# A retention layer and a SwiGLU block on one core: rounding of weights without a sign operation, and vector work moved between VectorE and ScalarE

## The chip, the cores and the metric

The kernel runs on one core of a Trainium2 chip. A core has five engines that run beside each other and wait for each other by semaphores: TensorE (PE; its weight loads are shown as PEld), VectorE (DVE), ScalarE (ACT), GpSimd (POOL) and SyncE (SP). Each works through its instructions in their order. ACT and SP also issue the kernel's DMAs, each from its own instruction queue, so that a DMA issue that has to wait holds up what stands behind it. The metric is the device time of one execution in microseconds (us); less is better.

## The reference

Eight batches with eight heads of 576 positions and 64 columns each. A retention step with decay makes x of 4608 rows and 512 columns, and a feed-forward block with 1536 hidden columns works on x:

```python
scores = scale * np.matmul(q, k.transpose(0, 1, 3, 2))
gamma = 1.0 - 2.0 ** (-5.0 - np.arange(H))
Dmat = np.where(rel >= 0, gamma[:, None, None] ** rel[None, :, :], 0.0)   # rel = row - column
x = bridge(np.matmul(scores * Dmat, v))          # (B,H,S,D) -> (B*S, H*D)
g, val = x @ w_gate, x @ w_val
out = (g / (1 + np.exp(-g)) * val) @ w_out
```

q, k and v are float32. The three weight matrices come as float64.

## The kernel before, in words

**Head pairs and ticks.** The retention is done for one pair of heads at a time: 32 pairs (8 batches x 4). A position's decay is split into a factor for the key, a mask and a factor for the query, in chunks of 64 positions, with a running state for the chunks before. `tick(t)` (L540) puts three pairs in flight. On PE it issues `own_values` of pair t-2 (L434), `new_states` of pair t-1 (L443), `earlier_values` of pair t-2 (L453, L457) and `scores` of pair t-1 (L464, L470). The rest of a tick is a list of pieces that is worked off at once or one by one at later steps (`go_on`): first `copies` (L481, ACT, the even chunks' new states out of PSUM) together with `keys` (L415, ACT, the two heads' keys times their decay), then `both` (L504 and L518, DVE, the outputs out of PSUM times the query's factor, into x), then the masks and states (L477 to L492, DVE), and last the two transposes of q and k of pair t (L411, DVE). `load(i)` (L254) brings a pair's q, k and v with 14 DMAs on SP's queue; it comes two ticks ahead, and its q and k need a place that the transposes of an earlier pair set free.

**Weights.** Each float64 weight of 1 MB is loaded by ACT's queue (`load_w`, three places) and rounded to float32 in two halves. `split` (L364, L365, on ACT) makes a scaled float32 out of the upper 32 bits and an integer out of the lower ones. `rounding` (L377 to L380, on DVE) shifts the first left by three bits, puts the sign bit back and adds the second. There are 36 halves. The order of loads and roundings is written out by hand (`order`, `round_until`, L332 and L901), and each rounding issues the next split.

**Tiles of tokens.** The first tile has 512 tokens; the four after it have 1024. The first is done plainly: `up0(f)` for twelve steps (L574, PE L579, Silu L583 on ACT, product L584 on DVE), with the banks in two pairs that alternate between steps, then `down0(f)` for twelve (L589, PE L591), the plain output steps, then `out0` (L594) copies the four banks out and issues four DMAs. Ticks 4 to 9 lie between the up steps and ticks 10 to 13 between the down steps. The other tiles use a scheme with fewer products: 26 up steps for each quarter of the hidden columns and 26 down steps, whose operands are sums of weight blocks and of x blocks. The tables UP, DOWN and OUT_SUMS list these sums. The sums of the output weights (`out_sums`, L641; POOL, line L617 and its neighbours) are formed during the first tile and stored (`dn<-rest`, L668). The groups that come up to step 10 are stored from SP's queue at once, those from step 11 on from ACT's; the latter are held back in a list until `stores_until` lets them go. The sums of the up weights are made during the second tile (`w_sums`: POOL L617 and L781, ACT L780) and stored by ACT (L814), then fetched in the later tiles. The second tile thus has more vector work than the later ones. Its bank results are read by DVE (L752), ACT (L749, L826) and POOL, and the products of the hidden values are made by L829, L832 and L833. The ticks of pairs 12 to 19 are spread over the steps of the second tile.

These functions and some definitions around them are printed here with the line numbers that the profile uses.

Of the kernel before, what the change touches and what calls it, by code (L numbers as in the profile page):

```python
# [12 lines left out]
F32 = mybir.dt.float32  # L13
# [9 lines left out]
def tables(gamma, scale, L):  # L23

    g, at = np.array(gamma), np.arange(L)  # L30
    both = lambda t: np.repeat(t, L, axis=0).reshape(-1, 2 * L, t.shape[1]).transpose(1, 0, 2).reshape(2 * L, -1)
    twice = lambda t: np.concatenate([t, t])
    parts = [twice((g[:, None] ** -at).T), twice((g[:, None] ** (L - at)).T),
             both(g[:, None] ** L), both(g[:, None] ** (2 * L)), both(scale * g[:, None] ** at),
             both((scale * g[:, None] ** at).reshape(-1, 2, L)[:, ::-1].reshape(-1, L))]
    return np.concatenate(parts, axis=1).astype(np.float32)

# [113 lines left out]
def kernel(  # L151
# [144 lines left out]
    table = tables(gamma, scale, L)  # L296
    tab = const.tile(list(table.shape), F32, name="tab")
    decays = nc.inline_tensor(table, name="decays").ap()
    NCOL = 2 * H + 2 * HP
    nc.sync.dma_start(out=tab[:, 0:NCOL], in_=decays[:, 0:NCOL])  # L300
    load(0)
    load(1)
# [6 lines left out]
    step = tab[:, 2 * H : NCOL]  # L309
# [46 lines left out]
    def split(j):  # L356

        i, f = halves[j]  # L360
        bits = bits_of(i, f)
        top, ulp = [rest[:, part_at + 512 * (2 * n + j % 2) : part_at + 512 * (2 * n + j % 2 + 1)] for n in range(2)]
        blocks = lambda a: a.rearrange("p (c m) -> p c m", m=P)
        nc.scalar.activation(out=blocks(top), in_=bits[:, :, :, 1].bitcast(F32), func=AF.Copy, scale=2.0 ** -112)  # L364
        nc.scalar.activation(out=blocks(ulp.bitcast(I32)), in_=bits[:, :, :, 0].bitcast(U32), func=AF.Copy, scale=2.0 ** -29)  # L365
        parts[j] = top.bitcast(I32), ulp.bitcast(I32)
        if f and j // 2 + RAWS < len(order):
            load_w(j // 2 + RAWS)

    def rounding(j):  # L370

        i, f = halves[j]
        dst = weights[i][1][f].bitcast(I32)
        top, ulp = parts.pop(j)
        nc.vector.tensor_scalar(out=dst, in0=top, scalar1=3, scalar2=None, op0=ALU.logical_shift_left)  # L377
        nc.vector.scalar_tensor_tensor(out=top, in0=top, scalar=-(1 << 31), in1=dst,
                                       op0=ALU.bitwise_and, op1=ALU.bitwise_or)
        nc.vector.tensor_tensor(out=dst, in0=top, in1=ulp, op=ALU.add)  # L380
        if j + 1 < len(halves):
            split(j + 1)

# [6 lines left out]


    st = {}

    def transposes(i):
        p = i % HP
        qk, kn, vt, last = loaded.pop(i)
        qT = qp.tile([P, S], F32, tag="qT", name="qT")
        st[i] = dict(qT=qT, kn=kn, v=vt, last=last)
        pieces = []
        if i < HP:  # L400

            for t, src, bank in ((qT, qk[0], bankA), (kT, kn, bankB)):
                for c in range(NFULL):
                    nc.tensor.transpose(bank[:, ts(c, P)], src[:, c].rearrange("p h d -> p (h d)"), ident)
                nc.scalar.copy(out=t[:, 0:CW], in_=bank)
            nc.tensor.transpose(bankC[:, 0:P], qk[1].rearrange("p h d -> p (h d)"), ident)
            for n, t in enumerate((qT, kT)):
                nc.scalar.copy(out=t[:, CW:S], in_=bankC[:, n * L : (n + 1) * L])
        else:
            for n, t in enumerate((qT, kT)):  # L410
                pieces.append(lambda n=n, t=t: nc.vector.transpose(out=t, in_=qk[:, n].rearrange("p j d -> p (j d)")))  # L411

        def keys():
            for hl in range(2):
                nc.scalar.activation(out=kn[:, :, hl, :], in_=kn[:, :, hl, :], func=AF.Copy,  # L415
                                     scale=key[:, 2 * p + hl : 2 * p + hl + 1])
            if i < RAWS:
                load_w(i)

        return [keys] + pieces  # L420

    straight, exchanged = [(slice(0, P), slice(0, P))], [(half[0], half[1]), (half[1], half[0])]
# [50 lines left out]
    def masked(i):  # L473
        p = i % HP

        def own():
            nc.vector.tensor_tensor(out=ret, in0=sc, in1=near[:, 2 * p : 2 * p + 2].unsqueeze(2).to_broadcast([P, 2, NFULL, L]),  # L477
                                    op=ALU.mult)

        def copies():  # L480
            nc.scalar.copy(out=even, in_=z[:, 0])  # L481

        def states():

# [7 lines left out]
            nc.vector.scalar_tensor_tensor(out=at[:, :, 1], in0=at[:, :, 0], scalar=step[:, p : p + 1], in1=even,  # L492
                                           op0=ALU.mult, op1=ALU.add)

        return [copies, own, states]

    def to_x(i):
# [3 lines left out]

        def both():

            nc.vector.tensor_tensor(out=dst(NC - 1, NC), in0=xr, in1=qry[:, p], op=ALU.mult)  # L504
            lo = 0
            while lo < NC - 1:
                end = lo + 1
                while end < NC - 1 and where(end)[0] == where(lo)[0]:
                    end += 1
                for r in range(2):  # L510
                    cs = range(lo + (lo + r) % 2, end, 2)
                    if cs:
                        n = len(cs)
                        for src, to in (exchanged if r and x else straight):
                            at = dst(cs[0] - r, cs[0] - r + 2 * n) if cs[0] - r >= lo and cs[-1] + 2 - r <= end else None
                            if at is not None:
                                at = at[to].rearrange("p (c r i) -> p c r i", r=2, i=L)[:, :, r]
                                nc.vector.tensor_tensor(out=at, in0=xo[src, cs[0] // 2 : cs[0] // 2 + n, r],  # L518
                                                        in1=(qry_odd if r and x else qry)[src, p].unsqueeze(1).to_broadcast([at.shape[0], n, L]), op=ALU.mult)
                            else:  # L520
                                for c in cs:
                                    nc.vector.tensor_tensor(out=dst(c, c + 1)[to], in0=xo[src, c // 2, r], in1=(qry_odd if r and x else qry)[src, p], op=ALU.mult)
                lo = end

        def dst(lo, end):
# [68 lines left out]
    def out0():  # L594
        for i, bank in enumerate(banks):
            o = rest[:, part_at + 512 * i : part_at + 512 * (i + 1)]
            if i < 3:
                nc.vector.tensor_copy(out=o, in_=bank)  # L598
            else:
                nc.scalar.copy(out=o, in_=bank)  # L600
            nc.scalar.dma_start(out=out[i * P : (i + 1) * P, :], in_=o)


    up, down = lines(UP), lines(DOWN)
# [36 lines left out]
    def out_sums(qd):  # L641
# [21 lines left out]
        def do(k, late):  # L663
            e = events[k]
            if e[0] is None:
                _, slot, i = e
                src, queue = view(slot), nc.scalar if late else nc.sync
                waiting.append((place.get(slot), lambda: queue.dma_start(out=dn_ops[i][:, qd * TB : (qd + 1) * TB], in_=src)))  # L668
# [258 lines left out]
    for m, f in enumerate(down_order):  # L927
# [69 lines left out]
```

## Time and profile before

| | us |
|---|---|
| median of 4 runs | 1086.05 (1084.39 to 1087.93) |
| the profiled execution | 1084.39 |
| its span, first to last instruction | 1082.7 |
| PE busy in it | 1041.8 (96%) |
| DVE busy | 678.4 (63%) |
| ACT busy | 266.9 (25%) |
| POOL busy | 408.4 (38%) |

The profile is of one execution. A row of groups gives line, engine, operation, what it writes and reads by the program's names (out<-in), its shapes (partitions x elements), how often it comes, and then busy us, mean ns of one, and the idle time of the engine just before, with what ended it. A row of the timeline gives start and duration in us, and in brackets the idle time before it and its releaser. A row of waits gives the sum in us, the number of waits and the longest. SPq and ACTq are the queues' own instructions, such as DMA issues. Matmul ends are modelled, so the busy time of PE says that matmuls followed each other and not that each ran at its peak.

### The profile page before, as it was taken

The page shows a single profiled execution, that of the slowest core. Times are in us where ns is not written, and L with a number is a line of the kernel's source. Part 1 is how long each engine was busy: PE and PEld are TensorE (multiplying, and loading weights), DVE is VectorE, ACT ScalarE, POOL GpSimd, SP SyncE. Part 2 cuts the span into 40 slices and gives each one's busy share as a digit, 9 for nine tenths or more (in the row PEclk, how much of TensorE's full clock was granted, in tenths as well). Part 3 has the DMA queues.
Part 4 walks back from the last instruction along what each step waited for, and adds up shares of the span by engine and source line. Part 5 has one row for each costly group of instructions (what it writes and reads, how often), then busy time and mean ns, then how long its engine had stood idle before and what let it go on. Part 6 is the DMA issues. An engine that isn't in the chain of part 4 may idle for free.

```text
span 1082.7 us, 21505 instructions
## 1 busy us (share of the span) xinstructions
PE 1041.8 (96%) x8420; PEld 853.5 (79%) x8420; DVE 678.4 (63%) x1123; ACT 266.9 (25%) x560; POOL 408.4 (38%) x357
## 2 busy tenths in 40 slices
PE   5899889999989899999999999999999999999998
PEld 4545445678878788888888888888888888888887
DVE  1788974976887976754646868535267464244644
ACT  3455421223242211223232111122221012231110
POOL 1002459675546402641215025622151375122505
PEclk9899999999999999999999999999999999999999
DMA  8989966666657779767667678554565555555653
GB/s 210 225 216 229 247 174 203 194 193 181 172 167 194 236 195 247 208 181 192 146 176 217 175 195 245 149 155 136 156 169 158 160 175 154 153 150 156 183 167 98
DMA packets 304212, 198.58 MB, mean 183 GB/s; under 512 B 219632, under 2 KB 247280, under 8 KB 304112
## 3 DMA queue, kind: packets, MB, share of 16 engines
q1 hardware_dynamic: 272512, 152.80, 54.1%
q10 hardware_dynamic: 31600, 44.41, 12.4%
q8 instruction: 67, 1.10, 0.5%
q14 instruction: 33, 0.27, 0.1%
HBM read 157.04 MB, written 40.11 MB: 182 GB/s over the span
## 4 chain that ended last, share of the span: by engine, by line
PE 73%; DVE 8%; DMA 7%; POOL 5%; issue 3%; SPq 2%; ACT 1%; ACTq 0%; DVEq 0%; POOLq 0%
PE bankC L811 11%; PE bankE L811 10%; PE bankA L811 10%; PE bankB L811 10%; PE bankE L850 6%; PE bankB L850 6%; PE bankC L850 6%; PE bankA L850 6%; POOL rest L617 2%; DVE rest L752 2%; PE outer L457 1%; DMA v<-in_v_dram 1%; POOL arena L617 1%; DMA rest<-in_moe_w_out_dram 1%; PE outer L434 1%
## 5 line engine op out<-in xcount | busy, mean ns | idle before, releaser
L752 POOL TENSOR_TENSOR rest<-rest 128x512 f32<-128x512 f32 x56 | 79.1, 1419 | 297.4 <-DVE rest L752 279.0
L826 ACT ACTIVATE io<-rest 128x256 f32<-128x256 f32 x180 | 75.0, 417 | 349.3 <-DVE rest L752 306.5
L811 PE MATMUL bankA<-rest,arena 128*128 128x256 f32 x544 | 129.1, 380 | 3.7 <-DVE rest L598 1.8
L811 PE MATMUL bankC<-rest,arena 128*128 128x256 f32 x544 | 129.3, 380 | 2.3 <-DVE rest L752 1.4
L617 POOL TENSOR_TENSOR rest<-rest 128x256 f32<-128x256 f32 (+1 forms) x86 | 84.1, 999 | 124.4 <-DVE rest L380 96.3
L617 POOL TENSOR_TENSOR arena<-arena 128x512 f32<-128x512 f32 (+1 forms) x72 | 114.6, 1605 | 32.4 <-DMA up<-arena 19.2
L811 PE MATMUL bankB<-rest,arena 128*128 128x256 f32 x512 | 121.6, 380 | 1.7 <-DVE arena L829 0.8
L811 PE MATMUL bankE<-rest,arena 128*128 128x256 f32 x512 | 121.5, 380 | 0.6 <-DVE rest L752 0.6
L811 PEld LDWEIGHTS bankA<-rest,arena 128*128 128x128 f32 x544 | 102.8, 190 | 19.8 <-issue 5.2
L811 PEld LDWEIGHTS bankC<-rest,arena 128*128 128x128 f32 x544 | 102.7, 190 | 17.7 <-issue 2.6
L833 POOL TENSOR_TENSOR arena<-rest,io 128x256 f32<-128x256 f32 x72 | 51.9, 726 | 167.1 <-ACT io L826 167.1
L811 PEld LDWEIGHTS bankB<-rest,arena 128*128 128x128 f32 x512 | 96.8, 190 | 16.3 <-POOL arena L781 1.2
L811 PEld LDWEIGHTS bankE<-rest,arena 128*128 128x128 f32 x512 | 96.9, 190 | 14.6 <-DVE rest L752 1.0
L752 DVE TENSOR_TENSOR rest<-bankC,rest 128x512 f32<-128x512 f32 x72 | 48.9, 687 | 66.0 <-PE bankC L811 45.9
L752 DVE TENSOR_TENSOR rest<-bankE,rest 128x512 f32<-128x512 f32 x72 | 48.8, 685 | 65.3 <-PE bankE L811 47.1
L752 DVE TENSOR_TENSOR rest<-bankB,rest 128x512 f32<-128x512 f32 x72 | 48.8, 686 | 64.7 <-PE bankB L811 47.0
L752 DVE TENSOR_TENSOR rest<-bankA,rest 128x512 f32<-128x512 f32 x72 | 48.8, 685 | 62.7 <-PE bankA L811 45.8
L829 DVE SCALAR_TENSOR_TENSOR arena<-rest,io 128x256 f32<-128x256 f32 x84 | 53.4, 640 | 12.6 <-ACT io L826 12.6
L850 PE MATMUL bankB<-arena 128*128 128x256 f32 x252 | 58.3, 381 | 0.0
L850 PE MATMUL bankA<-arena 128*128 128x256 f32 x252 | 58.1, 380 | 0.0
L850 PE MATMUL bankC<-arena 128*128 128x256 f32 x252 | 58.0, 380 | 0.0
L850 PE MATMUL bankE<-arena 128*128 128x256 f32 x252 | 57.9, 379 | 0.0
(150 smaller groups left out, 1650.0 us busy)
## 6 DMA issues: line engine op xcount, KB each, us to landing
arena<-up SPq DMA_DIRECT2D x234, 256.0 KB, 2.7
arena<-dn SPq DMA_DIRECT2D x104, 384.0 KB, 3.6
up<-arena ACTq DMA_DIRECT2D x78, 256.0 KB, 3.1
out_dram<-rest SPq DMA_DIRECT2D x32, 256.0 KB, 3.4
qk<-in_q_dram SPq DMA_DIRECT2D x112, 72.0 KB, 3.3
qk<-in_k_dram SPq DMA_DIRECT2D x112, 72.0 KB, 3.3
v<-in_v_dram SPq DMA_DIRECT2D x62, 128.0 KB, 3.1
kn<-in_k_dram SPq DMA_DIRECT2D x58, 128.0 KB, 3.2
```

The costliest lines, as they stand in the source:

```text
L434: m = nc.tensor.matmul(xo[half[hl ^ r * exchange(i)], c, r], s["v"][half[r], c, hl, :], ret[half[r], hl, c], start=(c == 0), stop=(c == 0) ...
L457: nc.tensor.matmul(xr[half[hl]] if c + 1 == NC else xo[half[hl ^ c % 2 * exchange(i)], c // 2, c % 2], state[half[hl], c, :], s["qT"][half ...
L617: eng.tensor_tensor(out=dst, in0=srcs[0], in1=srcs[1], op=ALU.add if op[0] == "add" else ALU.subtract)
L752: eng.tensor_tensor(out=at(op[1]), in0=at(op[2]), in1=at(op[3]), op=ALU.add if op[0] == "add" else ALU.subtract)
L811: nc.tensor.matmul(b[:, gv * TB : (gv + 1) * TB], w[:, gv, ts(c, P)], rhs[:, c, :], start=(opens and gv == 0 and c == 0), stop=(c == 1), s ...
L826: nc.scalar.activation(out=s, in_=src[:, 0:TB], func=AF.Silu, scale=-1.0 if negative else 1.0)
L829: return lambda: nc.vector.scalar_tensor_tensor(out=dst, in0=src[:, TB : 2 * TB], scalar=-1.0, in1=s, op0=ALU.mult, op1=ALU.mult)
L833: nc.gpsimd.tensor_tensor(out=dst, in0=src[:, TB : 2 * TB], in1=s, op=ALU.mult)
L850: nc.tensor.matmul(b[:, m * TB : (m + 1) * TB], lhs[:, qd, ts(m, P)], w[:, qd], start=(opens and qd == 0 and m == 0), stop=(qd == NQ - 1), ...
```

## The change

Four things are changed. In the rounding, the operation that puts the sign back is taken out; the split reads the upper bits through a parametric relu (`Prelu`) whose slope for negative values is 2^32, which after the shift by three bits leaves a one in the sign's place. At ticks 10, 11 and 12 (`vector`), which lie between the plain output steps and just behind them, the keys' scaling and the copy of the even states are done by DVE and not by ACT. For pairs 12 to 19 (`light`), ACT scales q with the query's factor ahead of the transposes, by a table of factors (`piece`) that is loaded with the small tables, and the outputs are then only copied to x, by ACT, where DVE multiplied them. In `out0` ACT copies the first two banks and DVE the last two, and the four DMAs come after the copies. The stores of the output weights' sums on ACT's queue are held back by three from the start, where they were all held back until the second down step.

```diff
+    half = [np.repeat(g.reshape(-1, 2), L, axis=1).T ** (lane % 32 + 32 * r) for r in range(2)]
+    pieces = scale * np.stack(half, axis=2).reshape(2 * L, -1)
...
-    NCOL = 2 * H + 2 * HP
+    NCOL = 2 * H + 4 * HP
...
-        nc.scalar.activation(out=blocks(top), in_=bits[:, :, :, 1].bitcast(F32), func=AF.Copy, scale=2.0 ** -112)
+        nc.scalar.activation(out=blocks(top), in_=bits[:, :, :, 1].bitcast(F32), func=AF.Prelu, scale=2.0 ** -112, alpha=2.0 ** 32)
...
-        nc.vector.scalar_tensor_tensor(out=top, in0=top, scalar=-(1 << 31), in1=dst,
-                                       op0=ALU.bitwise_and, op1=ALU.bitwise_or)
-        nc.vector.tensor_tensor(out=dst, in0=top, in1=ulp, op=ALU.add)
+        nc.vector.tensor_tensor(out=dst, in0=dst, in1=ulp, op=ALU.add)
...
+    def light(i):
+        return needed(1) - 2 <= i < needed(2) - 2
+    def vector(i):
+        return 10 <= i <= needed(1) - 2
...
+            if light(i):
+                def scale_q():
+                    src = qk[:, 0].rearrange("p (j r) d -> p r j d", r=2)
+                    for r in range(2):
+                        nc.scalar.activation(out=src[:, r], in_=src[:, r], func=AF.Copy, scale=piece[:, 2 * p + r : 2 * p + r + 1])
+                pieces.append(scale_q)
...
+                if vector(i):
+                    nc.vector.tensor_scalar(out=kn[:, :, hl, :], in0=kn[:, :, hl, :],
+                                            scalar1=key[:, 2 * p + hl : 2 * p + hl + 1], scalar2=None, op0=ALU.mult)
...
+        if light(i):
+            return [lambda: (keys(), pieces[0]())] + pieces[1:]
...
-            nc.scalar.copy(out=even, in_=z[:, 0])
+            (nc.vector.tensor_copy if vector(i + 1) else nc.scalar.copy)(out=even, in_=z[:, 0])
...
-            nc.vector.tensor_tensor(out=dst(NC - 1, NC), in0=xr, in1=qry[:, p], op=ALU.mult)
+            if light(i):
+                nc.scalar.copy(out=dst(NC - 1, NC), in_=xr)
+            else:
+                nc.vector.tensor_tensor(out=dst(NC - 1, NC), in0=xr, in1=qry[:, p], op=ALU.mult)
...
-                for r in range(2):
+                for r in range(0 if light(i) else 2):
...
+                if light(i) and lo % 2 == end % 2 == 0:
+                    nc.scalar.copy(out=dst(lo, end).rearrange("p (c r i) -> p c r i", r=2, i=L), in_=xo[:, lo // 2 : end // 2])
...
-            if i < 3:
-                nc.vector.tensor_copy(out=o, in_=bank)
-            else:
-                nc.scalar.copy(out=o, in_=bank)
-            nc.scalar.dma_start(out=out[i * P : (i + 1) * P, :], in_=o)
+            (nc.vector.tensor_copy if i > 1 else nc.scalar.copy)(out=o, in_=bank)
+        for i in range(4):
+            nc.scalar.dma_start(out=out[i * P : (i + 1) * P, :], in_=rest[:, part_at + 512 * i : part_at + 512 * (i + 1)])
...
-    behind = [len(OUT_SUMS)]
...
-                stores_until(behind[0] if late else 0)
+                stores_until(3 if late else 0)
...
-                stores_until(behind[0], new)
+                stores_until(3, new)
...
-        if m == 1:
-
-            behind[0] = 3
-            stores_until(3)
```

More of the change, by code (lines that the diff above doesn't have):

```diff
@@ L30, in tables @@
     g, at = np.array(gamma), np.arange(L)
+    lane = np.arange(2 * L)[:, None]
     both = lambda t: np.repeat(t, L, axis=0).reshape(-1, 2 * L, t.shape[1]).transpose(1, 0, 2).reshape(2 * L, -1)
     twice = lambda t: np.concatenate([t, t])
+    half = [np.repeat(g.reshape(-1, 2), L, axis=1).T ** (lane % 32 + 32 * r) for r in range(2)]
+    pieces = scale * np.stack(half, axis=2).reshape(2 * L, -1)
     parts = [twice((g[:, None] ** -at).T), twice((g[:, None] ** (L - at)).T),
-             both(g[:, None] ** L), both(g[:, None] ** (2 * L)), both(scale * g[:, None] ** at),
+             both(g[:, None] ** L), both(g[:, None] ** (2 * L)), pieces, both(scale * g[:, None] ** at),
              both((scale * g[:, None] ** at).reshape(-1, 2, L)[:, ::-1].reshape(-1, L))]
@@ L308 @@
     inv, key = tab[:, 0:H], tab[:, H : 2 * H]
-    step = tab[:, 2 * H : NCOL]
+    step = tab[:, 2 * H : 2 * H + 2 * HP]
+    piece = tab[:, NCOL - 2 * HP : NCOL]
     qry, qry_odd = [tab[:, NCOL + HP * L * n : NCOL + HP * L * (n + 1)].rearrange("p (h i) -> p h i", h=HP) for n in range(2)]
@@ L414, in keys @@
             for hl in range(2):
-                nc.scalar.activation(out=kn[:, :, hl, :], in_=kn[:, :, hl, :], func=AF.Copy,
-                                     scale=key[:, 2 * p + hl : 2 * p + hl + 1])
+                if vector(i):
+                    nc.vector.tensor_scalar(out=kn[:, :, hl, :], in0=kn[:, :, hl, :],
+                                            scalar1=key[:, 2 * p + hl : 2 * p + hl + 1], scalar2=None, op0=ALU.mult)
+                else:
+                    nc.scalar.activation(out=kn[:, :, hl, :], in_=kn[:, :, hl, :], func=AF.Copy,
+                                         scale=key[:, 2 * p + hl : 2 * p + hl + 1])
             if i < RAWS:
                 load_w(i)
+        if light(i):
+            return [lambda: (keys(), pieces[0]())] + pieces[1:]
         return [keys] + pieces
@@ L502, in both @@
         def both():
-            nc.vector.tensor_tensor(out=dst(NC - 1, NC), in0=xr, in1=qry[:, p], op=ALU.mult)
+            if light(i):
+                nc.scalar.copy(out=dst(NC - 1, NC), in_=xr)
+            else:
+                nc.vector.tensor_tensor(out=dst(NC - 1, NC), in0=xr, in1=qry[:, p], op=ALU.mult)
             lo = 0
@@ L522, in both @@
                                     nc.vector.tensor_tensor(out=dst(c, c + 1)[to], in0=xo[src, c // 2, r], in1=(qry_odd if r and x else qry)[src, p], op=ALU.mult)
+                if light(i) and lo % 2 == end % 2 == 0:
+                    nc.scalar.copy(out=dst(lo, end).rearrange("p (c r i) -> p c r i", r=2, i=L), in_=xo[:, lo // 2 : end // 2])
+                elif light(i):
+                    for c in range(lo, end):
+                        nc.scalar.copy(out=dst(c, c + 1), in_=xo[:, c // 2, c % 2])
                 lo = end
```

## The prediction

> **What bounds the kernel now.** I read the busy times by stage first, then who waited for whom on PE, then the timelines of the engines in the stretches where PE waits, and last SP's queue and POOL. The busy times by stage (columns: stretch, length, busy us of PE, PEld, DVE, ACT, POOL with instruction counts, granted clock, DMA share, GB/s):
>
> ```profile
> 0.00:40.00 40.00, 22.42 (x512) 20.10 (x512) 15.32 (x38) 15.26 (x36) 2.87 (x11) 0.87 0.93 217
> 40.00:118.00 78.00, 77.82 (x576) 38.14 (x570) 63.44 (x124) 37.78 (x67) 7.04 (x7) 1.00 0.92 228
> 118.00:150.00 32.00, 25.51 (x313) 13.17 (x312) 30.49 (x49) 15.28 (x28) 19.18 (x20) 0.95 0.75 195
> 150.00:200.00 50.00, 49.67 (x566) 26.29 (x566) 30.42 (x65) 3.98 (x9) 43.69 (x55) 1.00 0.62 181
> 200.00:256.00 56.00, 50.66 (x226) 42.18 (x227) 43.63 (x58) 15.64 (x33) 32.34 (x25) 1.00 0.65 189
> ...
> 298.00:375.00 77.00, 70.95 (x812) 60.56 (x811) 63.93 (x107) 24.28 (x54) 40.44 (x28) 1.00 0.70 192
> 375.00:1082.70 707.70, 702.88 (x5052) 616.61 (x5051) 399.54 (x636) 140.87 (x302) 238.42 (x194) 1.00 0.62 174
> ```
>
> PE is the bound: after 375 us it is busy 702.9 of 707.7. Whatever DVE or ACT saves there is worth nothing, and the change keeps that part as it is. Before 40 us PE waits for first loads (DMA share 0.93). What can be won lies in three stretches: 118 to 150 (6.5 us idle), 200 to 256 (5.3) and 298 to 375 (6.1). PE's waits name the causes:
>
> ```profile
> PE bankA L579 <- ACT io L583: 3.0, 1, 3.0
> PE bankE L591 <- DVE arena L584: 2.4, 1, 2.4
> PE outer L464 <- DVE kT L411: 1.9, 2, 1.7
> PE bankB L850 <- DVE state L492: 1.9, 1, 1.9
> ```
>
> The first is a late Silu. ACT's timeline and DVE's around it:
>
> ```profile
> 118.16 0.68 ACT L364 ACTIVATE rest<-rest 128x512 f32<-128x512 f32 x1 [0.64 <-DVE arena L380]
> ...
> 120.05 0.66 ACT L364 ACTIVATE rest<-rest 128x512 f32<-128x512 f32 x1 [0.65 <-DMA dn<-rest]
> ...
> 121.18 0.58 ACT L583 ACTIVATE io<-bankA 128x512 f32<-128x512 f32 x1
> ```
>
> ```profile
> 118.04 0.42 DVE L377 TENSOR_SCALAR rest<-rest 128x512 int32<-128x512 int32 x1
> 118.50 0.69 DVE L378 SCALAR_TENSOR_TENSOR rest<-rest 128x512 int32<-128x512 int32 x1
> 119.33 0.69 DVE L380 CUSTOM_DVE_ANT_0 rest<-rest 128x1024 uint16<-128x1024 uint16 x1
> ```
>
> Silu L583 of first-tile step 8 runs at 121.18, though PE finished that step at 111.8: it stands in ACT's queue behind splits (L364, L365) that wait for DVE's rounding. DVE has no idle time there. PE waits 2.98 us, and then its clock falls: the next eight matmuls take 5.40 us where the eight after them take 3.60, with a granted clock of 0.71 between 120 and 125. So this wait costs 4.8 us.
>
> **The change part by part.**
>
> *Rounding without L378.* By form, L378 is 24 x 730 ns and 12 x 863 ns = 27.9 us of DVE. A half of a weight now takes DVE 1.76 to 1.88 us (L377 at 114.40, 116.16, 118.04). Without L378 it is 0.42 + 0.69 + some 0.1 of waiting = 1.2 us; ACT's pair is no faster (L364 and L365 start 0.58 apart: 1.16 and a semaphore). So 0.6 to 0.7 us a half go. Between 57 and 118 some 20 halves precede the late Silu: 13 us against its lag of 9.4. DVE then waits for PE, not the reverse, and the 2.98 and the 1.8 of slow clock go. In 118 to 150 ten L378 take 9.4 of DVE's 30.5 busy us, so the waits at 141.7 to 149.9 (0.9 + 0.2 + 2.4 us) go too: PE would stand 2.98 + 1.8 + 3.5 = 8.3 us earlier at 150.
>
> *The parametric relu in place of a scaled copy (L364).* No row has this function. Functions don't show in the rows (Silu 128x512 from PSUM 585 ns, copy 590), so I take L364's 680 ns and no difference, between -0.02 and +0.02 us each. What could cost is a table. The trace holds two ACT_TABLE_LOAD, 1.283 us each, at 8.46 and 50.24, and none in the 90 us in which scaled copies and Silu alternate. [...]
>
> *What is late next.* Down-weights' sums (POOL L617) and their stores (SP L668). POOL's work from 155.00 to 202.7 has no idle time, and it is released by a store:
>
> ```profile
> 155.00 1.41 POOL L617 TENSOR_TENSOR rest<-rest 128x256 f32<-128x256 f32 x2 [7.12 <-DMA dn<-rest]
> ```
>
> ```profile
> 125.41 3.38 SPq L284 DMA_DIRECT2D qk<-in_q_dram  x4
> ...
> 143.87 2.94 SPq L284 DMA_DIRECT2D qk<-in_q_dram  x4
> ...
> 152.47 3.98 SPq L668 DMA_DIRECT2D dn<-rest  x8
> ```
>
> That store stands in SP's queue behind whole head-pair loads: 100.25 to 117.2, 125.4 to 137.9, 143.9 to 152.4. The first is paced by DMA (share 0.92 over 40 to 118) and won't move, or moves 1 to 2 us later, as the weight loads come sooner. The second took 12.5 us beside two weight loads; the third, with none, 8.5. Weight loads that are over sooner give the second 3 to 4 us. The third waited for the transposes (L411 at 142.4), which come some 10 us sooner, so it follows at once. POOL restarts at about 151: 4 us earlier, not 8.3 (bounds 0 and 8). The load after that (156.5 to 174.2, with kn landing at 173.5) follows SP in the same way, and PE's tick at 177.4 needs it.
>
> *VectorE for ScalarE at three plain ticks (L415, L481).* Six key scalings and three copies leave ACT. On DVE the copy from PSUM is 0.41 us by L518's 128x256; for the scaling no row fits, between 0.2 and 0.5 (L377, twice the size, 0.44), I take 0.3: 3 us in all, under 19.6 us of idle DVE in 150 to 200. The new wait: DVE takes the keys ahead of a tick's masks, states and transposes, so these 6 us now stand behind kn's landing, where only ACT stood before. It costs nothing until PE needs those states. With PE 8 us ahead and kn 4 ahead, PE waits at 177's tick: a second reason for 4.
>
> *Stores after three (behind).* They leave ACT's queue at step 11 and not after down step 1. What stood behind them there, the copy L481 (13.9 and 9.2 us waited), is now on DVE. POOL has places enough then and never waited after 155. 0, from -1 to +1.
>
> *Outputs of the first tile.* PE waited 1.76 us for L598, DVE's copy of bank A, held up by sums L617 at 199.22. ACT is idle from 181.7, so bank A comes free at once. But DVE's next sums sit idle 2.21 us until 205.46 for the last store, and PE's steps after 208 hang on them: this lets PE run into the next wait. I count 0.3 of the 1.8. Four DMAs stay on ACT, now behind DVE's two copies; up stores L814 follow them as before.
>
> *Second tile's ticks.* Off DVE, each of eight pairs: 0.21 + 2 x 0.41 = 1.03 us (L504, L518). On ACT: two scalings of 128x288 (L415's 0.51 for 128x256; 0.55 each) and copies of 0.23 + 0.59 (L408, L749): 1.9 us a pair. ACT is busy 24.3 of 77 us in 298 to 375, so they lie beside DVE's work; without that cover a Silu, and a bank, would be 1.9 late. DVE runs without a pause in front of three PE waits, at 298.6 and 305.9, at 356.1, and at 372.0, with one pair's products in each: 0.8 + 0.7 + 0.7 = 2.2 us. Bounds 0 (the transposes then wait for the scaling, or POOL L781 is late as before) and 3.1.
>
> **Sum.** 4.0 + 0.3 + 2.2 = 6.5 us. The profiled execution took 1084.39 us (span 1082.7 and 1.7 around it), 1.7 below the median of the runs, 1086.05. So 1077.9 by that execution and 1079.5 for the median.
>
> **Rivals.**
> - *Full gain.* POOL and SP follow the whole way (a wait shorter by 8 at 155), and ACT's early copies of banks A and B shorten 200 to 256: 8.3 + 1.5 + 2.5 = 12.3, 1073.7. For it: DMA share is only 0.62 to 0.75 after 118. Against: the load at 100 to 117 is held by DMA.
> - *The feeders don't move.* Store and loads keep their times, POOL ends at 202.7 as before; only the second tile is won: 1086.05 - 2 = 1084, down to no gain.
> [...]
>
> **Chances.** Main case 0.52 (1076 to 1083), full gain 0.20 (1070 to 1076), feeders unmoved 0.20 (1083 to 1087), slower 0.08. About 0.3% (3.3 us) is what a measurement of this kernel can tell from no change, so faster is below 1082.8: 0.50 + 0.20 + 0.06 = 0.76; same 0.16; slower 0.08. The range 1072.5 to 1084.5 leaves out about 0.07 below and 0.13 above.
>
> **What would show it.** Right: no wait on L583 near 118 and a full clock there; no L584 wait; PE's first L811 at about 196 to 198 and not 201.6; POOL's wait for a store ending near 151; L411 and L492 waits shorter by about 0.8. Wrong: more than two ACT_TABLE_LOAD; an ACT split of over 0.75 us; PE waiting in the tick near 170 for states, keys or v by more than 4 us; new PE waits on ACT's copies in the second tile.

## The result, and the profile after

| | before | changed |
|---|---|---|
| median, us | 1086.03 (56 runs) | 1086.69 (35 runs) |
| ratio, 95% interval | | 0.9998 (0.9988 to 1.0009) |
| the profiled execution, its span | 1084.39, 1082.7 | 1086.98, 1085.3 |
| POOL: row of sums begins, ends | 155.0, 202.7 | 153.7, 202.4 |
| kn and v of load 11 landed | 173.5 and 174.0, 174.6 and 175.1 | 177.2 and 178.2, 178.8 and 179.3 |

No difference, where 1079.5 was forecast. Lines are numbered anew in the changed kernel: up steps L612 (L579 before), plain output steps L624 (L591), second tile's up steps L842 (L811; L843 in some runs), own values L459 (L434), new states L468 (L443), earlier values L478 and L482 (L453 and L457), states L512 to L517 (L487 to L492), transposes L430 (L411), DVE's keys L435, copies L506 (L481), POOL's sums L648 (L617), stores of sums L699 (L668), loads L288, L269, L295 (L284, L265, L291). The same stages of the changed kernel, with columns as in the prediction:

```profile
118.00:150.00 32.00, 32.00 (x464) 18.00 (x463) 20.15 (x40) 10.98 (x21) 15.47 (x20) 1.00 0.69 171
150.00:200.00 50.00, 36.73 (x402) 20.77 (x401) 21.89 (x54) 1.15 (x2) 41.92 (x56) 0.86 0.59 175
200.00:256.00 56.00, 54.69 (x233) 43.56 (x232) 46.84 (x61) 15.81 (x32) 33.01 (x24) 1.00 0.64 189
...
298.00:375.00 77.00, 72.97 (x814) 61.98 (x812) 59.15 (x92) 29.52 (x71) 40.11 (x28) 0.98 0.67 180
```

PE is now busy without a pause in 118 to 150 (25.5 of 32 before) at full clock, so the rounding did what was predicted. In 150 to 200 it lost 13.3 us, where it had lost 0.3. PE's longest waits in 150 to 260 name the loss, and DVE's timeline around it shows what DVE stood at:

```profile
PE outer L459 <- DVE ret_last L510: 11.9, 1, 11.9
PE outer L482 <- DVE state L517: 1.2, 1, 1.2
```

```profile
158.09 0.42 DVE L506 COPY even<-inner 128x256 f32<-128x256 f32 x1 [2.01 <-PE inner L495]
177.25 0.58 DVE L435 TENSOR_SCALAR kn<-kn,tab 128x256 f32<-128x256 f32 x1 [18.74 <-DMA kn<-in_k_dram]
178.18 0.50 DVE L435 TENSOR_SCALAR kn<-kn,tab 128x256 f32<-128x256 f32 x1 [0.35 <-DMA kn<-in_k_dram]
```

PE stands at tick 12 from 168.5 to 180.4, since DVE stands at the keys of pair 11 for 18.7 us, with the masks of pair 10 behind them. After the wait PE's clock is down (columns as in the stages):

```profile
176.00:180.00 4.00, 0.00 (x0) 0.00 (x0) 2.40 (x8) 0.47 (x1) 3.91 (x7) 0.50 0.84 222
180.00:184.00 4.00, 2.39 (x72) 2.20 (x74) 3.89 (x8) 0.00 (x0) 3.92 (x6) 0.50 0.61 198
184.00:188.00 4.00, 4.00 (x71) 3.38 (x70) 2.17 (x7) 0.00 (x0) 3.83 (x6) 0.59 0.77 252
```

PE's 6.4 busy us between 180 and 188 ran at a clock of 0.5 to 0.59: about 2.9 us more are lost. The first loads of an execution end at different times, so I count from PE's first up step (40.2 before, 40.4 changed). Tick 10 begins 114.2 us after it before and 105.0 changed, 9.2 earlier; tick 13 begins 147.0 and 153.7, 6.7 later (9.2 - 11.9 - 1.2 - 2.9 = -6.8). The second tile begins 4.8 later, but its first 56 us lose less (idle time in 200 to 256: 5.3 before, 1.3 now), and at the wait for kT near 306 (end of that wait: 267.4 and 268.2) only 0.8 is left. Behind that wait a slower clock costs the changed kernel another 1.6 (last section).

POOL's row of sums begins with

```profile
153.66 1.66 POOL L648 TENSOR_TENSOR rest<-rest 128x256 f32<-128x256 f32 x2 [8.11 <-DVE state L514]
```

The row names a state on DVE, but a store of sums had landed at 153.53, 0.13 us ahead, just as one had landed at 154.87 in the trace of before, where the row names it.

So there are two questions: what makes kn late, and why PE's earliness is worth nothing even where it isn't lost at once. SP's issues of load 11 (start, length from the first to the last issue, count), before:

```profile
156.54 5.48 SPq L284 DMA_DIRECT2D qk<-in_q_dram  x4
164.41 5.45 SPq L284 DMA_DIRECT2D qk<-in_k_dram  x4
170.03 1.57 SPq L265 DMA_DIRECT2D kn<-in_k_dram  x2
```

In the changed kernel, first two rows of load 10, which comes just before, then load 11:

```profile
142.15 2.07 SPq L288 DMA_DIRECT2D qk<-in_q_dram  x4
...
146.51 0.98 SPq L269 DMA_DIRECT2D kn<-in_k_dram  x2
...
155.20 6.80 SPq L288 DMA_DIRECT2D qk<-in_q_dram  x4
164.56 8.92 SPq L288 DMA_DIRECT2D qk<-in_k_dram  x4
173.59 1.07 SPq L269 DMA_DIRECT2D kn<-in_k_dram  x2
```

Load 10 issues its kn 4.4 us after its first q. Load 11 begins 1.3 us sooner than before the change, but takes 18.4 us to its kn (13.5 before). SP's waits in 150 to 180, first before, then changed, say for what:

```profile
SPq L284 <- DMA dn<-rest: 7.5, 4, 2.5
```

```profile
SPq L288 <- DMA dn<-rest: 15.3, 6, 4.0
```

They are waits for stores of sums that ACT issues, those of up step 11 and of the first four down steps; the later ones go out from SP again (from 174.3 before). In the built program the DMAs of SP and ACT (983 in the trace of before and as many in that of the changed kernel) take eight semaphores in turn, numbered 0 to 7 here, and each of SP's late issues of load 11 waits for the DMA that had its semaphore last. The semaphores of load 11's eight issues of q and k:

```
before             2 5 1 5 2 6 7 0
changed            2 6 3 7 4 1 5 0
stores on SP       4 5 6 7 0 1 2 3
```

(The last row is an experiment below.) Each number skipped is a store of ACT that has taken its turn in between: 15 stores before, 23 in the changed kernel. So six of SP's eight issues wait for a store (four before), the stores for sums, and POOL makes its sums at its own pace. In the changed kernel's trace these six late issues (160.17, 161.68, 164.56, 168.02, 170.89, 173.16) start within 0.1 us of the landing of such a store. The part that moves the copies and keys off ACT is what changes the turns: with that part alone they are those of the changed kernel, and without it 2 6 3 5 2 6 7 0 (both runs below). Stores of ACT had stood behind those copies, for which ACT waited 13.9 and 9.2 us in the trace of before.

### The profile page after: what moved, and what is told of

It reads as the page before. It is cut to its first block, busy times and chain, and to the rows that moved or that the text cites. A ratio compares the mean times of both kernels' runs of the same rounds, so it can differ in the third digit from the quotient of the medians.

```text
span 1085.3 us, 21477 instructions
## 1 busy us (share of the span) xinstructions
PE 1043.3 (96%) x8420; PEld 857.8 (79%) x8420; DVE 645.0 (59%) x1063; ACT 275.6 (25%) x588; POOL 401.7 (37%) x357
## 4 chain that ended last, share of the span: by engine, by line
PE 81%; DVE 5%; POOL 4%; DMA 4%; issue 3%; SPq 2%; ACT 1%; ACTq 0%; DVEq 0%; POOLq 0%
PE bankE L842 11%; PE bankA L842 11%; PE bankB L842 10%; PE bankC L842 10%; PE bankE L881 6%; PE bankB L881 6%; PE bankC L881 6%; PE bankA L881 6%; PE bankA L612 2%; PE bankC L612 2%; PE bankB L612 2%; PE outer L482 2%; DVE rest L783 2%; POOL rest L648 2%; PE bankE L612 2%
## 5 line engine op out<-in xcount | busy, mean ns | idle before, releaser
L842 PE MATMUL bankC<-rest,arena 128*128 128x256 f32 x544 | 129.3, 380 | 1.4 <-DVE rest L783 1.4
L842 PE MATMUL bankA<-rest,arena 128*128 128x256 f32 x544 | 129.0, 380 | 0.8 <-DVE rest L783 0.8
L648 POOL TENSOR_TENSOR arena<-arena 128x512 f32<-128x512 f32 (+1 forms) x72 | 114.3, 1600 | 38.1 <-DMA up<-arena 19.1
L648 POOL TENSOR_TENSOR rest<-rest 128x256 f32<-128x256 f32 (+1 forms) x86 | 79.7, 948 | 127.9 <-DVE rest L384 91.3
L842 PE MATMUL bankB<-rest,arena 128*128 128x256 f32 x512 | 122.2, 382 | 1.2 <-DVE arena L860 0.8
L842 PE MATMUL bankE<-rest,arena 128*128 128x256 f32 x512 | 122.3, 382 | 0.0
L842 PEld LDWEIGHTS bankC<-rest,arena 128*128 128x128 f32 x544 | 102.7, 190 | 16.8 <-issue 2.6
L842 PEld LDWEIGHTS bankA<-rest,arena 128*128 128x128 f32 x544 | 103.0, 190 | 16.3 <-issue 1.7
L842 PEld LDWEIGHTS bankB<-rest,arena 128*128 128x128 f32 x512 | 97.6, 191 | 15.8 <-DVE arena L860 1.2
L842 PEld LDWEIGHTS bankE<-rest,arena 128*128 128x128 f32 x512 | 97.4, 191 | 13.7 <-DVE rest L783 0.3
```

Of the source, the lines that this page charges most:

```text
L648: eng.tensor_tensor(out=dst, in0=srcs[0], in1=srcs[1], op=ALU.add if op[0] == "add" else ALU.subtract)
L842: nc.tensor.matmul(b[:, gv * TB : (gv + 1) * TB], w[:, gv, ts(c, P)], rhs[:, c, :], start=(opens and gv == 0 and c == 0), stop=(c == 1), s ...
```

## The experiments

Theory A: DVE's order is the cause, keys ahead of masks. Theory B: load 11 is late in itself, through the stores between its issues. Each ratio is to the kernel before on the same chip and at the same time: the first four kernels ran on one chip, the next four on a second, the other six later in pairs. A trace is of one execution, and not always of one near the median.

**Keys last.** In this kernel pair 12's scaling of q comes after its transposes, so that factor is missing in its output.

```diff
-        pieces.append(lambda: (copies(), keys()))
+        late_keys = lo <= t < hi and vector(t)
+        pieces.append(lambda: (copies(), None if late_keys else keys()))
...
         pieces.extend(new)
+        if late_keys:
+            pieces.append(keys)
```

> The changed kernel with one move: at ticks 10 to 12 the keys' scaling stays on DVE but comes last among the tick's pieces, behind masks, states and transposes. Theory A (DVE's order: keys(11) stand ahead of the masks and states and hold them until kn lands): PE's wait of 11.9 us at 168.5 goes, about 1075 us. Theory B (the load itself is late: kn(11) lands at 177.2 and v(11) at 179.3 because SP's issues wait for ACT's stores): PE's first matmuls of the tick run, and then it waits for keys and v until about 179.5; only the 1.0 us from there to 180.4 and the 1.2 us of the next wait go: 1084 to 1085 us.

1084.2 us, ratio 0.9977 (0.9964 to 0.9990). PE's timeline:

```profile
176.85 0.44 PE L468 MATMUL inner<-v,kn 64*64 64x64 f32 x2 [10.62 <-DMA v<-in_v_dram]
```

The masks and states are done at 160.7, PE's own values start the tick at 165.5, and then PE waits 10.6 us for v of load 11, which DVE's order can't touch. Theory A falls as the main cause; B's 1084 to 1085 holds.

**No keys or copies on DVE.**

```diff
-        return 10 <= i <= needed(1) - 2
+        return False
```

> The changed kernel without its second part: keys and copies of ticks 10 to 12 are on ACT as before; rounding, stores after three, outputs of the first tile and second tile as in the changed kernel. Theory A: nothing stands on DVE ahead of the masks, the whole wait goes: about 1075 us. Theory B: in the built program load 11 now has about as many stores of ACT between its issues as before the change (its q and k parts wait on semaphores 2 6 3 5 2 6 7 0; before 2 5 1 5 2 6 7 0, changed 2 6 3 7 4 1 5 0), so kn lands at 170 to 173 and v at 172 to 175, and PE, ready at 168.5, waits 4 to 7 us: 1079 to 1082 us.

1082.3 us, 0.9963 (0.9950 to 0.9977). B's load came as expected (kn 171.4, v 172.3 to 172.9), but PE didn't wait for it, since it stood earlier: 10.4 us at 152.6 for ret_last. ACT's timeline shows the releaser:

```profile
155.56 6.04 ACTq L699 DMA_DIRECT2D dn<-rest  x9
161.72 0.37 ACT L506 COPY even<-inner 128x256 f32<-128x256 f32 x1 [24.69 <-DMA dn<-rest]
```

With the copies back on ACT they stand behind the stores, and the masks wait for the copies. Before the change this wait of ACT was there too (13.9 us for L481), but PE came 9 us later and didn't feel it. Neither theory had named it. It is again the stores of POOL's sums that hold what PE needs, but through ACT's queue and not through load 11.

**Stores on SP, behind load 11.**

```diff
-                src, queue = view(slot), nc.scalar if late else nc.sync
+                src, queue = view(slot), nc.sync
...
-                stores_until(3 if late else 0)
+                stores_until(behind[0] if late else 0)
...
+        if m == 1:
+            behind[0] = 3
+            stores_until(3)
```

> The changed kernel with all stores of the output weights' sums on SP's queue and held back until the second down step, so that they stand behind load 11 and none lies between its issues; keys stay at the head of DVE's pieces. Theory A: the keys still stand ahead of the masks, but how long depends on kn; if the load's time doesn't matter apart from it, 1086 us. Theory B: the load takes 8 to 9 us as load 10 did, kn lands near 165, PE doesn't wait at 168.5: 1073 to 1076 us.

SP's timeline, and PE's longest wait in 150 to 260:

```profile
153.34 2.85 SPq L288 DMA_DIRECT2D qk<-in_q_dram  x4
156.25 2.36 SPq L288 DMA_DIRECT2D qk<-in_k_dram  x4
158.72 0.98 SPq L269 DMA_DIRECT2D kn<-in_k_dram  x2
```

```profile
PE bankA L843 <- ACT rest L781: 5.7, 1, 5.7
```

The load takes 5.4 us to its kn, v lands at 162.7 to 163.3, and the stall of tick 12 is gone although the keys still stand first on DVE: B. The second tile begins 152.6 us after the first up step, 8.8 sooner than before. The time is nevertheless 1083.6 us, 0.9968 (0.9954 to 0.9983), not 1073 to 1076: PE waits at 196.3 for the change of tiles. ACT's copy of bank A stands behind output DMAs that wait, by the same eight semaphores, for the last stores of sums (one goes out at 197.69, a store with its semaphore having landed at 197.61). The traced execution was the fastest of 22, 1076.5 us: its first up step came 3.5 us sooner than in the trace of before, and from there to the end it is 4.4 us shorter. So even here half of the 8.8 is lost again.

**Rounding alone**, on the kernel before.

```diff
-        nc.scalar.activation(out=blocks(top), in_=bits[:, :, :, 1].bitcast(F32), func=AF.Copy, scale=2.0 ** -112)
+        nc.scalar.activation(out=blocks(top), in_=bits[:, :, :, 1].bitcast(F32), func=AF.Prelu, scale=2.0 ** -112, alpha=2.0 ** 32)
...
-        nc.vector.scalar_tensor_tensor(out=top, in0=top, scalar=-(1 << 31), in1=dst,
-                                       op0=ALU.bitwise_and, op1=ALU.bitwise_or)
-        nc.vector.tensor_tensor(out=dst, in0=top, in1=ulp, op=ALU.add)
+        nc.vector.tensor_tensor(out=dst, in0=dst, in1=ulp, op=ALU.add)
```

> The kernel before with the first part alone: no sign operation, parametric relu in the split. No keys on DVE. PE is then 8.3 us earlier at 150, as in the changed kernel. Theory A: nothing takes it back, 1086.0 - 8.3 = 1077.7 us. Theory B: load 11 has the same stores between its issues as before the change, v lands at 171 to 175 and PE waits 3 to 7 us of the 8.3 for it: 1081 to 1085 us.

1086.0 us, 0.9995 (0.9980 to 1.0010). B's range was missed by 1 us, A's by 8, and B's wait wasn't there either: v landed at 169.8 and 170.4, and PE began tick 12 at 175.3 without a wait. It waited 5.3 and 1.1 us at tick 11 for masks and states that stood behind ACT's copy (19.6 us idle behind stores), then 2.2 us for the first tile's copies: the gain is gone by the second tile.

**The second tile's part alone**, and **keys and copies alone**, each on the kernel before: the changed kernel with its other parts undone, `light` or `vector` left as it is and the other one switched off.

```diff
-        return needed(1) - 2 <= i < needed(2) - 2
+        return False
```

> The kernel before with the second tile's part alone: for pairs 12 to 19 ACT scales q and copies the outputs to x. By the prediction's step (one pair's products, 0.7 to 0.8 us, off each of three PE waits) 2.2 us, 1083.7 us. By the changed kernel's trace, where those waits shrank only in part (PE's idle time in 298 to 375 from 6.05 to 4.0 us, of which some is another wait), 1 to 2 us: 1084 to 1085. If ACT becomes late for a bank or for the transposes: 1086 or more.

1083.2 us, 0.9964 (0.9951 to 0.9976), a larger gain than expected. Its trace, of the second slowest execution of 22 (1086.1 us), shows little of it: from the wait for a hidden product near 254 to the end of that for kT the time is 53.1 us, 53.7 before; the waits for kT (1.7) and near 372 (1.9) are unchanged.

> The kernel before with the second part alone: keys and copies of ticks 10 to 12 on DVE, rounding as before, so that PE is as late at 150 as before. In the built program load 11 has the same stores of ACT between its issues as in the changed kernel. Theory B (the load is late through those stores): v(11) lands about 179 instead of 175 and PE, ready at 177.4, waits 2 to 3 us there: 1087 to 1090 us. Theory A (only DVE's order): DVE holds the masks until kn lands at about 177, PE waits 2 to 4 us for ret_last: 1088 to 1090 us. If the move is harmless without the rounding: 1085 to 1086 us. The traces tell A from B by what PE's new states wait for last, keys or v, and when they land.

1087.1 us, 0.9999 (0.9984 to 1.0013). kn landed at 177.4 and 178.3, v at 179.0 and 179.4, as in the changed kernel, and PE waited 4.0 us at 176.4. So the late load comes from this part alone; with PE not yet early it costs a wait of 4 us and not 12, and no time that can be measured. Between A and B this run doesn't decide, as both forecast such a wait.

**Stores on SP, and no keys or copies on DVE** (both edits above).

> The changed kernel with the stores on SP behind load 11 (as in the run with all stores on SP) and with keys and copies on ACT again: ACT's queue holds no store, so its copies can't be late, and no key stands on DVE ahead of a mask. Theory B: as the run with the stores on SP, less its 1.6 us wait for states at 166: 1082 to 1083 us; PE then waits at 196 to 205 for POOL's last sums and their stores, which don't come sooner. Theory A has nothing left to hold PE: 1074 us.

1083.2 us, 0.9967 (0.9955 to 0.9980), as B had it. PE's two longest waits in 150 to 260:

```profile
PE bankC L843 <- POOL arena L648: 4.4, 1, 4.4
PE bankA L843 <- ACT rest L781: 3.0, 1, 3.0
```

PE reaches the second tile at 189.7 and then waits 11 us in pieces up to 220. POOL runs from 153.4 to 201.3 without a pause: sums of the output weights first, then those that the second tile's up steps need.

**A third of the sums on DVE.** Beside POOL's from the first down step, from the fifth, and from the seventh, on the kernel with both edits above. The cut shows the last of the three; the others differ in the table of steps.

```diff
-    groups = [(qd, group) for qd in range(NQ) for group in out_sums(qd)]
+    groups = [(qd, group) for qd in range(NQ) for group in (out_sums(qd, nc.vector) if qd == NQ - 1 else out_sums(qd))]
...
+        for qd, n in ((1, 1), (2, {6: 2, 7: 2, 8: 2, 9: 1, 10: 1, 11: 1}.get(m, 0))):
+            for g in [g for g in groups if g[0] == qd][:n]:
+                groups.remove(g)
+                g[1](m < 4)
```

> The run before this one, with the last third of the output weights' sums on DVE and not on POOL, one group of it beside one of POOL's at each of the first nine down steps. If POOL's 47 us of sums without a pause (148.6 to 196 in the run with the stores on SP) are what the gain is lost to at the change of tiles, the wait of 5.7 us at 196 and some of the waits after it go: 1073 to 1078 us. If the change of tiles is held by DVE's sums of x or by something else: 1082 us as without it, or more, as DVE takes some 14 us of work.

1092.6 us, 1.0058 (1.0037 to 1.0079). A sum on DVE waited 25.1 us, to 169.6, for a place whose store stood behind load 11 on SP; the masks stood behind that sum, and PE waited 18.4 us.

> The run with the stores on SP and keys and copies on ACT, with the last third of the output weights' sums on DVE, now only from the fifth down step on (two groups a step), so that they stand behind the masks of ticks 10 and 11 and behind load 11 and wait for no store that this load holds up. If POOL's unbroken row of sums is the next bound (its waits of 4.4, 3.0 and smaller ones after PE reaches the second tile at 189.7, 11 us in all), POOL ends some 20 us sooner, these waits go and the second tile starts at about 190 as without it: 1072 to 1077 us. If the bound there is something else (DVE's sums of x, the first loads of the second tile): 1082 to 1084 us as without it.

1077.9 us, 0.9928 (0.9901 to 0.9954). POOL's sums of the output weights end at 172.1 (196.5 without the sharing), and PE has no wait above 0.8 us between 180 and 256. One is left at 167.5, for pair 11's transpose of k, again behind such a sum:

```profile
PE outer L489 <- DVE kT L430: 7.8, 1, 7.8
```

> As the run with the late sums on DVE, but DVE's third of the sums begins at the seventh down step (2, 2, 2, 1, 1, 1 groups) and not at the fifth, behind tick 12. In that run PE waited 7.8 us at 167.5 for pair 11's transpose of k, which stood on DVE behind sums that waited for places whose stores stood behind load 11. Here no sum stands ahead of that transpose: the wait goes, with some 1.7 us of slow clock after it: 1067 to 1072 us. If another wait takes its place at 190 to 200, since DVE's sums now meet its sums of x: 1074 to 1079.

1072.5 us, 0.9894 (0.9873 to 0.9916), the fastest: 1.1% below the kernel before. Its stages:

```profile
150.00:200.00 50.00, 48.70 (x460) 29.33 (x459) 36.07 (x76) 7.52 (x15) 25.53 (x32) 1.00 0.75 224
200.00:256.00 56.00, 51.71 (x232) 42.88 (x230) 42.19 (x55) 19.07 (x41) 34.84 (x27) 1.00 0.63 180
```

PE loses 1.3 us in the stage where the changed kernel lost 13.3, and 4.3 in the next, as the second tile now begins at 188.3. POOL is busy 25.5 us in the first of them and not 41.9.

**The fastest with keys and copies on DVE again.**

> The same with keys and copies of ticks 10 to 12 on DVE, as in the changed kernel. With load 11 free of stores, DVE's order can cost only what kn(11) lands later than the copies before it: PE then waits 1 to 2 us for states at about 166, as in the run with the stores on SP: the same as the run before this one to 2 us more. If DVE's order were the main cause of the stall (theory A) some 10 us more.

1075.5 us, 0.9923 (0.9899 to 0.9946): waits of 0.9, 0.8 and 1.2 us for states and masks. This is what DVE's order costs by itself, about 3 us, not 10.

**What the two useful parts are worth.** First the changed kernel without the second tile's part, then the fastest with the old rounding, then the fastest without the second tile's part (`light` returns False, as above).

> The changed kernel without the second tile's part (no scaling of q and no copies to x on ACT); rounding, keys and copies on DVE, outputs and stores as changed. If the second tile's part is worth as much inside the changed kernel as alone (3.1 us by the medians), and its gain pays for what the stall of 12 us costs: 1089 to 1091 us. If its gain was lost as the second tile starts later anyway: 1086 to 1087 us as the changed kernel.

1086.7 us, 0.9995 (0.9973 to 1.0017): nothing lost. The stall of tick 12 was there (11.5 us), so the part's gain did not pay for it.

> The fastest version with the rounding as before (sign operation, scaled copy). If the rounding's gain is real and was only taken back by the stall and POOL's sums: PE is 8 to 9 us later at 150 and nothing takes that back, 1079 to 1082 us. If PE's earlier arrival is worth little in itself (the next bound lies just behind): 1072 to 1076 us.

1079.0 us, 0.9942 (0.9920 to 0.9965): over the fastest, 6.6 us by the medians and 5.2 by the ratios, as the two ran on different chips. From the first up step to the end the traces differ by 5.3 (1039.8 and 1034.5). The waits for the Silu and the hidden product are back:

```profile
PE bankE L626 <- DVE arena L619: 2.4, 1, 2.4
PE bankA L614 <- ACT io L618: 2.1, 1, 2.1
```

It is at the edge of the first expectation, and far from the second.

> The fastest version without the second tile's part. As the prediction had it, 2.2 us slower: 1074.7 us; as the traces' waits in 256 to 375 show it (0.7 us of idle time), 1073; as the part alone measured it, 1075.5 to 1076 us.

1073.0 us, 0.9896 (0.9873 to 0.9918): 0.5 us over the fastest by the medians, 0.2 by the ratios. That is nearest to what the waits show, but with six runs each the interval is some 2.4 us either way, and 2.2 isn't shut out.

## Why the prediction was wrong, step by step

- *Rounding, up to 150: right.* DVE's busy time fell by 10.9 us in 40 to 118 and by 10.3 in 118 to 150, the waits for the Silu and for L584's product are gone, the clock there is 1.00, and PE is 9.2 us earlier (8.3 predicted). In every trace with the new rounding tick 10 begins 105.0 to 105.3 us after the first up step, with the old one 114.2 to 116.2. The gain is worth 5 to 7 us where nothing takes it back.
- *Parametric relu: right.* 36 x 675 ns (680 predicted), two ACT_TABLE_LOAD of 1.283 us as before. The 0.08 for a slower kernel stood for more of these loads; there were none.
- *"POOL restarts at about 151": wrong in size.* 153.7, or 1.5 us earlier counted from the first up step, and its row ends at 202.4, now with a pause of 3.1 us at 194.9. I had load 10 wait only for the transposes. It began at 142.15, right behind stores of sums on SP, of which the last waited for POOL, and the trace of before has it so too: 143.87, behind a store that went out at 143.19 with POOL's newest sum. POOL's places wait for stores, stores for loads on SP, loads for stores: this chain hangs on itself and hardly on PE. That was the rival "the feeders don't move", which I had given 0.20.
- *"The load after that ... follows SP in the same way": the step that failed.* It began 1.3 us earlier and its kn landed 3.7 later, so PE, ready at 168.5, met a v that came at 179.3, and waited 11.9 us. I had taken its 17.7 us in the trace of before as a length and not asked why load 10 needed half of that. It has pauses: the waits in SP's queue for ACT's stores, 7.5 us, stood in the trace of before, and 15.3 became of them.
- *Keys and copies on DVE: right place, wrong cause, wrong price.* The wait of tick 12 is where I put it, priced as a part of the "4". It is 11.9 us with 1.2 and about 2.9 of slow clock behind it. DVE's order is the releaser that the profile names; with the keys last PE waits 10.6 us for v. What I did not see is that moving the copies off ACT lets ACT's stores take more of the semaphores' turns ahead of load 11.
- *Stores after three: 0, not shown false.* The run with keys and copies alone holds the stores back as before and has the turns 2 6 3 7 4 1 5 0 too, so the late load isn't due to this edit. No run undoes it alone.
- *Outputs of the first tile: not settled.* L598's wait of 1.8 us is gone, but PE also came 4.8 us later.
- *Second tile, 2.2: more than the traces show.* The wait near 300 fell from 0.92 to 0.41 us; that for kT stayed at 1.7, since in both traces DVE stands 1.7 us, ahead of the transpose of k, for a sum of POOL (L781, now L812) that itself waits for ACT (7.1 and 7.7 us), which is the lower bound that I had named; that near 372 stayed (1.86, now 1.81), with a load of dn as its releaser. So 0.5 to 0.7 us, with which the last run agrees, though it can't tell it from 2.2. Why this part alone gave 0.36% stays open. The mean clock of its timed runs was 0.9930 against 0.9913 of before, which by the slope over the runs of before (0.65 us for 0.001) is 1.1 us of the 3.1; 1.3 or so has no place. That slope is no more than a correlation.

The sum had the right gain in front and no price for what came of it. Tick 12 cost 16.0 us against the gain of 9.2. Most of the 6.7 us by which PE was then late came back in 200 to 256, where PE had lost 5.3 us before and now lost 1.3. That POOL's sums set the time there is shown for the kernels with the stores on SP, by the runs that shorten POOL's row: 1083.2 us without the sharing, 1077.9 and 1072.5 with it. For the changed kernel it is argued from these, as the profile of before names POOL in only 1.3 of those 5.3 us.

Until that row was shortened, PE's arrival at the second tile decided little. Counted from the first up step it came at 166.2 in the changed kernel, 163.7 with the keys last, 164.9 with no keys on DVE, 162.7 with the rounding alone and 152.6 with the stores on SP; the medians are 1086.7, 1084.2, 1082.3, 1086.0 and 1083.6.

## What to carry to other kernels

Before counting an engine's earliness as a gain, ask of each transfer that it needs next why it takes as long as it does: a load with pauses between its issues waits for something, and where two queues draw on the same semaphores, look for waits of one for the other's transfers even where no data connects them (here SP waited 7.5 us for stores of ACT before, and 15.3 in the changed kernel). The releaser that a profile names for a wait is the last of a chain; put it last in its order and see who is waited for then. And a compute engine off the path that works 47 us without a pause next to a stage that gets shorter can be the next bound, so shorten or share its row first, and keep what is shared behind whatever the critical engine needs next.

## What the runs showed of the hardware that was not expected

The clock falls after some of PE's waits of about 2 us and not after others of the same length, so that one execution costs 1.7 us more than another. From the end of the wait near 372 to the end of the span the traces have either 708.8 us (nine of the sixteen, before and changed among them) or 710.5 to 710.8 (the other seven, among them no keys on DVE, rounding alone and second tile alone). The wait in front was 1.6 to 2.3 us in the first group and 1.9 to 2.4 in the second. In the second group the granted clock is 0.5 for 3.41 us behind the wait, in the first it stays at 1.00. After kT's wait of 1.7 the stretch to the end of the wait near 372 is 66.3 before, at a clock of 1.00, and 67.9 in the changed kernel, with 0.5 for 3.41 us from 310.2.

In each of the traces of before and changed, the changes of the granted clock lie whole multiples of 3.41 us apart. Between 42 and 1080 us there are three falls to 0.5: for 3.41 us from 122.1 before, and in the changed kernel for 13.65 from 173.6 and for 3.41 from 310.2. In the 3.41 us ahead of them PE was busy for 0.43, 0 and 1.70 us. After three other such stretches of these two traces, with 1.45, 1.55 and 1.72 us, the clock stayed at 1.00, so they give no border. For kT's wait, 1.71 us in both traces, what differs is where it lies: in the changed kernel within one stretch (306.75 to 310.16, PE busy for 1.70), before across two that meet at 306.45 (2.85 and 2.26). Two other waits of nearly one length differ in the same way. One of 2.37 us, all of it in the first row, from the run with sums on DVE from the fifth step (columns as in the stages):

```profile
364.40:367.80 3.40, 1.03 (x5) 0.68 (x4) 3.36 (x6) 0.59 (x1) 0.98 (x1) 1.00 0.83 284
367.80:371.20 3.40, 3.40 (x9) 2.68 (x8) 1.44 (x2) 0.00 (x0) 0.00 (x0) 0.50 0.97 344
```

One of 2.28 us, in both rows, from the run with the stores on SP and no keys on DVE:

```profile
369.00:372.40 3.40, 1.67 (x8) 1.13 (x6) 3.29 (x6) 0.76 (x2) 2.26 (x2) 1.00 0.81 209
372.40:375.80 3.40, 2.85 (x13) 2.57 (x14) 2.79 (x4) 0.00 (x0) 0.00 (x0) 1.00 0.87 287
```

PE was busy for 1.03 of the 3.40 us ahead of the clock of 0.50, and for 1.67 and 2.85 where it stayed at 1.00. That a wait of this length is followed by half clock more easily when it lies within one stretch is an estimate from these four waits.

This is a part of why runs of one kernel differ by more than many of the edits here: the timed runs of the kernel before lie between 1082.9 and 1091.8, and over its 57 runs on the second chip 0.001 less of mean clock goes with 0.65 us more. The first loads may be another part: in the sixteen traces the first up step begins between 35.9 and 41.6 us.
